# A recurrent attention followed by an MLP mixer: one more pair of weights formed in the second weave, and new orders for the first two

## The chip, the cores and the metric

The kernel runs on one core of a Trainium2 chip. A core has engines that run side by side, each with its own queue of instructions in order: TensorE (PE, matmuls; PEld is its loading of weights), VectorE (DVE), ScalarE (ACT), GpSimd (POOL) and SyncE (SP, which here issues nearly all DMA transfers). They wait for each other through semaphores only. The metric is the time of one execution on the device in microseconds (us), given as the median of several runs.

## The reference

For 4 batches of 768 tokens with 8 heads of 48 channels, a recurrence over time gives `y`; its heads side by side are `x` (768 x 384 per batch). Then an MLP mixer works along the tokens and along the channels:

```python
for t in range(S):
    cur = einsum(u * k_t, v_t);  y[t] = r_t @ (state + cur)
    state = w_t[:, None] * state + outer(k_t, v_t)
h  = relu(x.T @ w_tok1) @ w_tok2;   z = x + h.T       # 768 -> 256 -> 768 along the tokens
out = z + relu(z @ w_ch1) @ w_ch2                     # 384 -> 1536 -> 384 along the channels
```

The weights come as 64-bit floats and are turned into 32-bit ones on the chip.

## The kernel before

*Units and batches.* The attention of a batch is done in three units of 256 tokens (units 0 to 11 for four batches). A unit turns its decays into running products (`ends`, `begins`), scales keys and queries by them, forms grams of 64-token chunks on PE, carries the state from chunk to chunk, and copies its result into `x`. `own_u[a]` (L444, with `by_u` L327, the instruction of L329) multiplies the keys of one of four head pairs by `u` on ACT, for the diagonal of the gram.

*The mixing.* After the attention of a batch comes its mixing. For batch 0 (`mixing`, L880): `back` (L893; the matmuls of L896 and the residual add of L898 on DVE), `turn` (L903; three transposes on PE, L907, and a copy to `xT` by ACT, L909), `up` (L916; L931 and, for the last third of the tokens, L927, with a rectifying copy by ACT, L934 or L928) and `down` (L936; L942 and an add on DVE, L946). `up(s, jt)` works on the tokens of turns 2s and 2s+1. Batches 1 to 3 use `exact_mixing` (L635), whose matmuls take operands split in two shorter parts (L735, L737, L742 up; L753, L754, L755 down), with the first rectified part written by L717 on ACT.

*Conversion.* Each of the 64-bit channel weights comes as pairs of blocks; a pair is `load` (L257, SP), `signs` (L269, ACT), `exponent` (L260, DVE), `raise_two` (the power of two, L263, ACT), `mantissa` (L266), `add` (L272), and `put` (L275, L282), the last three on DVE.

*Forms.* The later mixings need each pair of channel weights in split forms. `splits(kind, n)` (L572) gives six pieces for pair `n` of the first (`kind` 0) or second (`kind` 1) weights: `up` (L575, ACT), `rest` (L579, DVE), `low` (L582, ACT), `store` (L588 or L590, a DMA on SP), `join` (L594, DVE), `joint` (L597, ACT). There are six pairs of each kind. The third form lies in DRAM and is loaded back into a ring of ten places (`load_third`, L615). The forms of the mixing's activations (`z_high`) lie in the room of the second channel weights, so L717 cannot write before the last `store` and `joint` of kind 1.

*The order.* Everything up to the first `back` is one list written out by hand (L1030). From there, four weaves follow, one per batch (L1135). A weave joins the mixing of a batch with the attention of the next and with what is left of the weights. Each of these is a list of pieces in a fixed order, a stream. A string of digits in `WEAVES` (L50) says from which stream the next piece is taken (`interleaved`, L1010), and `strict` (L103) makes every engine, SP among them, issue its instructions in that order. So a piece that waits for something holds up all that comes after it on its engine. In weave 0 the digits mean: 0 the mixing of batch 0, 1 to 3 the units 3, 4 and 5, 4 the rest of the conversion and the forms. In weave 1: 0 and 1 the mixing of batch 1 and the joins of its transposes, 2 to 4 the units 6 to 8, 5 the forms that are left. `weights_in_turn` (L1108) cuts the list of forms in two: the last 6 x `AFTER` pieces go into weave 1.

```python
    late = [e for n in range(HALF) for e in splits(1, n)]
    return first[:1] + each[1] + ... + formed + late[:1] + late[6:7] + late[1:6] + late[7:-6 * AFTER], late[-6 * AFTER:]
AFTER = 2
```

*Loads of keys.* `load_rk(i)` (L170) brings the keys and then the queries of a unit, each in two halves of 48 rows (the DMA of L168, on SP). The one for unit 3 stands near the end of the list by hand, behind two pairs of raw weights.

Of the kernel before, what the change touches and what calls it, by code (L numbers as in the profile page):

```python
# [47 lines left out]
LEAST, MOST = 2.0 ** -40, 2.0 ** 40  # L48
MID = 3 * G // 4 * SEG1
WEAVES = [  # L50
    "440140440440000440401041114001004140004404040411441110104414014401041041014144110144140104404110140444000414141004140414"
    "442044444104440214401040404000424420404012404240024022400042242242420242244422044040204442200422044422000202443003334030"
    "43040303443332342344343300343243434334034343243304404300344342403333",
    "050000022220000505250502225052502205522502012100010252000000220200002000200002200200020002000220300000300200330033003030"
    "033000000000030000023330330302000033303033003330000000101103000003300040020400000000204300000040044000444000404443304444"
    "4044040000000440404000400000044003040004040000300444000000000000",
    "204240000022033204220000433322344240400000044440010001100404440000000000044000004040040000400044004000400400404055550000"
    "050505000500000000055000450055450005055055540550500045005050500001101050505606000000000006000400000660606666065606060000"
    "066005066050606660000606000605600000606000600006060660006000000000000000",
# [6 lines left out]
def rwkv6_then_mixer(  # L66
# [1041 lines left out]
    def weights_in_turn():  # L1108
# [8 lines left out]
        late = [e for n in range(HALF) for e in splits(1, n)]  # L1117
        return first[:1] + each[1] + sum(each[2:], []) + stored + formed + late[:1] + late[6:7] + late[1:6] + late[7:-6 * AFTER], late[-6 * AFTER:]

    AFTER = 2  # L1120
    flagged = []

    def verdict():
# [153 lines left out]
```

## Time and profile before

| | |
|---|---|
| median of 3 runs | 483.54 us (482.88 to 484.61) |
| the profiled execution | 484.18 us, of which the span from first to last instruction is 482.4 us |
| mean clock granted to TensorE | 0.989 |
| DMA | 83.77 MB, 174 GB/s on average |

A profile shows for each engine the time that its instructions took (busy), and for idle time what released the engine. Rows of the form `start, duration, engine, line, operation, out<-in` stand for one instruction or for several alike (`xN`); a note in brackets gives the idle time ahead of it and what ended it. The rows by stage give, after the length of a stretch, the busy time of PE, PEld, DVE, ACT and POOL with the number of instructions, the clock granted to PE, and the share and rate of DMA. A 32-bit matmul leaves two records, one of shorter operands leaves one. Weave 0 runs from about 50 to 167 us, weave 1 to about 276 us.

### The profile page before, as it was taken

What the parts mean: (1) busy time and instruction counts of PE and PEld (TensorE: products, weight loads), DVE (VectorE), ACT (ScalarE), POOL (GpSimd) and SP (SyncE); (2) the same over time, 40 slices, a digit from 0 to 9 for tenths busy, and PEclk for the clock granted to TensorE, in tenths of its full rate; (3) what the DMA queues carried; (4) which work ended last, traced back from release to release, by engine and by line L of the source; (5) the groups of instructions that cost most, each with busy time, mean ns of one, the idle gap of its engine ahead of it and who ended that gap; (6) DMA issues with size and microseconds to landing.
All of it is one profiled execution on the core that took longest, in us unless ns stands there. A gap on an engine that the chain in (4) does not pass through costs nothing.

```text
span 482.4 us, 12668 instructions
## 1 busy us (share of the span) xinstructions
PE 464.6 (96%) x5298; PEld 407.8 (85%) x5298; DVE 336.4 (70%) x478; ACT 254.4 (53%) x587; POOL 59.3 (12%) x58
## 2 busy tenths in 40 slices
PE   3799999999999999999999999999999999999995
PEld 2686688866697668999999969999999979999994
DVE  7999899798788778757856398767856365235331
ACT  5789866753779666354546255365545244034040
POOL 1000000000000001230504002140413003032030
PEclk9889999999999999999999999999999999999998
DMA  8965927760674566774737644395605622436321
GB/s 300 336 200 205 271 96 244 254 209 33 190 239 136 187 176 209 211 225 150 228 129 242 224 146 127 116 262 182 194 23 177 219 77 83 123 91 206 90 81 56
DMA packets 49408, 83.77 MB, mean 174 GB/s; under 512 B 4864, under 2 KB 40576, under 8 KB 49344
## 3 DMA queue, kind: packets, MB, share of 16 engines
q1 hardware_dynamic: 49056, 82.80, 54.5%
q8 instruction: 43, 0.70, 0.6%
q14 instruction: 21, 0.17, 0.1%
q10 hardware_dynamic: 288, 0.10, 0.1%
HBM read 71.87 MB, written 11.01 MB: 172 GB/s over the span
## 4 chain that ended last, share of the span: by engine, by line
PE 95%; ACT 2%; DMA 1%; issue 0%; SPq 0%; DVE 0%; DVEq 0%; ACTq 0%
PE h_ps L942 10%; PE ends_ps L735 8%; PE ends_ps L742 8%; PE ends_ps L737 8%; PE o_ps L753 8%; PE o_ps L755 8%; PE o_ps L754 8%; PE z_ps L931 7%; PE h_ps L658 5%; PE gram L313 4%; PE z_ps L927 3%; PE h_ps L689 3%; PE kv_ps L361 3%; PE y_ps L397 3%; PE y_ps L376 2%; PE k_ps L343 2%
## 5 line engine op out<-in xcount | busy, mean ns | idle before, releaser
L728 POOL TENSOR_TENSOR z_high<-z_high 128x384 fp32r<-128x384 f32 x48 | 58.0, 1212 | 406.5 <-ACT z_high L717 188.9
L761 DVE SCALAR_TENSOR_TENSOR x<-o_ps,x 128x384 f32<-128x384 f32 x35 | 19.1, 555 | 55.5 <-PE o_ps L755 55.5
L717 ACT ACTIVATE z_high<-ends_ps 128x384 fp32r<-128x384 f32 x48 | 23.5, 489 | 58.1 <-PE ends_ps L742 58.1
L735 PE MATMUL ends_ps<-x_forms,forms 128*128 128x384 f32 x216 | 50.4, 341 | 0.0
L742 PE MATMUL ends_ps<-z_more,forms 128*128 128x384 f32 x216 | 50.2, 340 | 0.0
L737 PE MATMUL ends_ps<-x_forms,ring 128*128 128x384 f32 x216 | 49.3, 337 | 0.0
L942 PE MATMUL h_ps<-wch,z 128*128 128x384 f32 x144 | 48.6, 490 | 0.0
L724 DVE SCALAR_TENSOR_TENSOR z_high<-ends_ps,z_high 128x384 fp32r<-128x384 f32 x48 | 26.5, 553 | 31.0 <-ACT z_high L717 30.6
L753 PE MATMUL o_ps<-forms,z_high 128*128 128x384 f32 x140 | 47.9, 342 | 0.0
L755 PE MATMUL o_ps<-forms,z_high 128*128 128x384 f32 x140 | 47.2, 337 | 0.0
L754 PE MATMUL o_ps<-ring,z_high 128*128 128x384 f32 x140 | 47.1, 337 | 0.0
L497 ACT ACTIVATE before<-state,to_end 112x48 f32<-112x48 f32 x132 | 33.2, 323 | 18.2 <-DVE state L512 16.0
L942 PEld LDWEIGHTS h_ps<-wch,z 128*128 128x128 f32 x144 | 26.6, 190 | 16.8
L742 PEld LDWEIGHTS ends_ps<-z_more,forms 128*128 128x128 f32 x216 | 38.9, 188 | 0.3 <-DVE z_more L630 0.2
L735 PEld LDWEIGHTS ends_ps<-x_forms,forms 128*128 128x128 f32 x216 | 38.2, 188 | 0.7
L737 PEld LDWEIGHTS ends_ps<-x_forms,ring 128*128 128x128 f32 x216 | 38.6, 188 | 0.0
L931 PE MATMUL z_ps<-xT,wch 128*128 128x256 f32 x144 | 31.8, 380 | 0.0
L931 PEld LDWEIGHTS z_ps<-xT,wch 128*128 128x128 f32 x144 | 27.1, 190 | 3.8
L720 ACT ACTIVATE z_high<-z_high 128x384 fp32r<-128x384 f32 x48 | 25.2, 526 | 3.3
L753 PEld LDWEIGHTS o_ps<-forms,z_high 128*128 128x128 f32 x140 | 26.3, 188 | 0.2
L754 PEld LDWEIGHTS o_ps<-ring,z_high 128*128 128x128 f32 x140 | 26.3, 188 | 0.0
L755 PEld LDWEIGHTS o_ps<-forms,z_high 128*128 128x128 f32 x140 | 26.3, 188 | 0.0
(194 smaller groups left out, 929.4 us busy)
## 6 DMA issues: line engine op xcount, KB each, us to landing
ring<-third SPq DMA_DIRECT2D x144, 192.0 KB, 3.2
raw<-in_w_ch_dram SPq DMA_DIRECT2D x16, 512.0 KB, 5.0
rk<-in_rk_dram SPq DMA_DIRECT2D x36, 192.0 KB, 5.2
near<-in_near_dram SPq DMA_DIRECT2D x8, 768.0 KB, 4.9
w<-in_w_dram SPq DMA_DIRECT2D x10, 520.5 KB, 4.0
vt<-in_v_dram SPq DMA_DIRECT2D x12, 384.0 KB, 4.4
out_dram<-x SPq DMA_DIRECT2D x17, 192.0 KB, 2.3
third<-forms SPq DMA_DIRECT2D x12, 192.0 KB, 3.3
```

The lines of the kernel that those rows point to most:

```text
L497: act.mul(t[:ROWS, a], state[bt, g][:ROWS, a], by_last(c, j)[:, a:a + 1])
L720: act.mul(z_form(jt, 2), z_form(jt, 0).bitcast(f32), 1.0 / BASE)
L724: dve.scalar_tensor_tensor(z_form(jt, 1), a, 0.0, z_form(jt, 0).bitcast(f32), op0=ALU.max, op1=ALU.subtract)
L728: pool.tensor_add(z_form(jt, 2), z_form(jt, 2).bitcast(f32), z_form(jt, 1).bitcast(f32))
L735: pe.matmul(a, up[m], xf[0][:, m], start=m == 0, stop=False)
L737: pe.matmul(a, low[:, m], xf[1][:, m], start=False, stop=False)
L742: pe.matmul(banks["a", jt], joint, xf[2][:, m], start=False, stop=m == 2)
L753: pe.matmul(a, z[0], up, start=first, stop=False, skip_group_check=True)
L754: pe.matmul(a, z[1], held[bt, s, half, 1, jt], start=False, stop=False, skip_group_check=True)
L755: pe.matmul(a, z[2], joint, start=False, stop=last, skip_group_check=True)
L931: pe.matmul(ps, now["wch1"][:, m, ts(jt, 128)], xT[:, m, ts(s, SEG)], start=(m == 0), stop=(m == DM // 128 - 1))
L942: pe.matmul(ps, zs[s][:, jt, ts(n, 128)], now["wch2"][:, jt, :], start=(jt == 0), stop=(jt == NJ - 1))
```

## The change

`AFTER` goes from 2 to 3: pair 3 of the second channel weights, the third from the end, has its six pieces in weave 1 instead of weave 0. The strings of weaves 0 and 1 are replaced as a whole (that of weave 0 has 302 digits instead of 308, that of weave 1 310 instead of 304; weaves 2 and 3 are untouched). No piece is added or removed.

```diff
 WEAVES = [
-    "440140440440000440401041114001004140004404040411441110104414014401041041014144110144140104404110140444000414141004140414"
...
+    "114444104104040410004140000400004414400001444004414111110414014404040014140414110441144010144440101014440011441040411001041"
...
-    "050000022220000505250502225052502205522502012100010252000000220200002000200002200200020002000220300000300200330033003030"
...
+    "000255552050020225500050020220552050550125022520510252125002000000200000020020000002020000000202200200022020000330300000"
...
-    AFTER = 2
+    AFTER = 3
```

At the start of weave 0 this changes the order on two engines. On PE it stays `back` 0 to 2, `turn` 0, `back` 3, `turn` 1, `back` 4, `turn` 2, `back` 5, `turn` 3, `up`. On the others:

| engine | before | after |
|---|---|---|
| ACT | signs 1, power 1, copy of turn 0, turn 1, signs 2, copy of turn 2, own_u[0] of unit 3, copy of turn 3, power 2, own_u[1], [2], [3], first rectified copies | own_u[0] of unit 3, signs 1, power 1, own_u[1], [2], copy of turn 0, turn 1, own_u[3], signs 2, copy of turn 2, turn 3, first rectified copies, power 2 |
| DVE | put 0, add of back 0, exponent 1, back 1, mantissa 1, back 2, add 1, back 3, back 4, put 1, exponent 2, back 5 | put 0, exponent 1, back 0, mantissa 1, back 1, add 1, back 2, back 3, put 1, back 4, back 5, exponent 2 |

Later in weave 0, units 4 and 5 run somewhat earlier beside the matmuls of `down` and `up` (their `tokens`, `carry` and grams move by a few matmuls of L942 and L927), and unit 5 is finished before the last two pieces of `down`. In weave 1 the six pieces of pair 3 stand near the start, behind the loads of unit 6 and among the first matmuls of L658; pairs 4 and 5 follow. On SP the store of pair 3 then comes ahead of the first four loads of the ring.

More of the change, by code (lines that the diff above doesn't have):

```diff
@@ L50 @@
 WEAVES = [
-    "440140440440000440401041114001004140004404040411441110104414014401041041014144110144140104404110140444000414141004140414"
-    "442044444104440214401040404000424420404012404240024022400042242242420242244422044040204442200422044422000202443003334030"
-    "43040303443332342344343300343243434334034343243304404300344342403333",
-    "050000022220000505250502225052502205522502012100010252000000220200002000200002200200020002000220300000300200330033003030"
-    "033000000000030000023330330302000033303033003330000000101103000003300040020400000000204300000040044000444000404443304444"
-    "4044040000000440404000400000044003040004040000300444000000000000",
+    "114444104040410004140000400004414400001444004414111110414014404040014140414110441144010144440101014440011441040411001041"
+    "444040420414440424100242440201244222024404444040420022244220442402424204042204420242442000400402224434034004404042300034"
+    "03304334033434343423333333332033400344300343304243344424300033",
+    "000255552050020225500050020220552050550125022520510252125002000000200000020020000002020000000202200200022020000330300000"
+    "023033300000003303000030003233030300330330233003303230003000002300110034100400000004000000400444034004004040000434340004"
+    "0344044440040040400004004000004044300040000400004000440000000000000000",
     "204240000022033204220000433322344240400000044440010001100404440000000000044000004040040000400044004000400400404055550000"
```

## The prediction

> **What bounds the kernel now.** I read the page first, then who waited for whom on PE, then the busy time by stage.
>
> ```profile
> span 482.4 us, 12668 instructions
> ...
> PE 464.6 (96%) x5298; PEld 407.8 (85%) x5298; DVE 336.4 (70%) x478; ACT 254.4 (53%) x587; POOL 59.3 (12%) x58
> ...
> PE 95%; ACT 2%; DMA 1%; issue 0%; SPq 0%; DVE 0%; DVEq 0%; ACTq 0%
> ...
> PE gram L313 <- DMA rk<-in_rk_dram: 8.4, 1, 8.4
> PE kv_ps L504 <- ACT before L497: 1.2, 2, 1.0
> PE k_ps L343 <- PE kv_ps L504: 0.8, 1, 0.8
> PE h_ps L896 <- ACT h L891: 0.6, 1, 0.6
> PE y_ps L397 <- ACT seen L385: 0.5, 1, 0.5
> PE h_ps L689 <- ACT z_high L682: 0.2, 1, 0.2
> ...
> 60.00:70.00 10.00, 10.00 (x52) 8.75 (x50) 9.90 (x13) 7.08 (x15) 0.00 (x0) 1.00 0.38 126
> ...
> 165.00:187.00 22.00, 22.00 (x262) 14.35 (x262) 16.91 (x23) 13.06 (x24) 0.00 (x0) 1.00 0.64 187
> ```
>
> PE is the chain (95% of it). All its waits together are 11.7 us, and all but the last belong to the first 50 us, which the change leaves alone: on every engine the first moved instruction stands behind them. In the two woven stages (about 50 to 167 and 167 to 276 us) the rows by stage show PE busy for 10.00 of 10.00 and 22.00 of 22.00 us. Busy can hide gaps between pipelined matmuls, so I looked at their spacing:
>
> ```profile
> 58.99 10.36 PE z_ps L931 x48
> ...
> 101.85 10.52 PE h_ps L942 x32
> ```
>
> 0.216 us each for 128x256 and 0.329 for 128x384, the same wherever they stand. So there is hardly a wait to take away: what the new order can win on PE is about the 0.2 us of L689. What it can lose is open: a wait that PE is now given is lost to the end, because nothing behind it has slack on PE.
>
> The Trainium skill, "Perfetto Trace Analysis", Identifying the Most-Contended Engine, says that matmul busy time tells little of headroom and that the share of weight loading should be read instead. By that rule the stage of 165 to 187 us (weight loading 14.35 of 22) would have up to 7.65 us to win; the even spacing above speaks against it, and it enters only as a rival below.
>
> **The change, part by part.** *The moved pair.* AFTER = 3 takes the six pieces of pair 3 of the second channel weights (up L575, rest L579, low L582, store L590, join L594, joint L597) out of the first weave and puts them into the second.
>
> ```profile
> L575 ACT ACTIVATE forms<-wch 128x768 fp32r<-128x768 f32 x12 | 10.0, 839 | 2.7 <-DVE starts L427 2.6
> L579 DVE TENSOR_TENSOR forms<-wch,forms 128x768 fp32r<-128x768 f32 x12 | 11.2, 944 | 0.6 <-ACT forms L575 0.6
> L582 ACT ACTIVATE wch<-forms 128x768 f32<-128x768 f32 x6 | 5.0, 841 | 2.6 <-DVE forms L579 2.2 <-PE h_ps L942 0.3
> L594 DVE TENSOR_TENSOR forms<-forms,wch 128x768 fp32r<-128x768 f32 x6 | 5.7, 954 | 1.0 <-ACT wch L582 0.9
> ...
> 180.90 0.37 SPq L590 DMA_DIRECT2D third<-wch  x1
> ...
> DMA to landing us min/median/max: 2.4/3.6/5.5
> ...
> 188.88 0.47 ACT L717 ACTIVATE z_high<-ends_ps 128x384 fp32r<-128x384 f32 x1
> ```
>
> That is 3 x 0.84 = 2.5 us of ACT, 0.94 + 0.95 = 1.9 us of DVE and one store of 384 KB. In the first weave they lay beside PE, so taking them out wins nothing. In the second, between 165 and 187 us, ACT goes from 13.06 to 15.6 and DVE from 16.91 to 18.8 of 22 us: they fit. What would be late if they did not is the first L717: its tile lies in the room of the second channel weights, so it waits for the last store, issued at 180.90; with the 3.6 us that the six stores of L590 took in the median it landed at 184.5, 4.4 us before 188.88. An extra pair put wholly ahead of that store costs 0.84 + 0.94 + 0.84 = 2.6 us, and with join and joint 4.4: even so L717 is not late, and I take 0. (If that cover were gone, the same 4.4 us would be the price.) On SP the store goes ahead of the first loads of the ring (L621) and delays their issue by its own 0.37 us.
>
> *The order of PE, DVE and SP elsewhere.* Both programs have the same matmuls, and 36 places in each where a run of 64-row matmuls gives way to full ones; the new order on PE costs 0. On DVE the exponent of conversion 1 (L260) now precedes the first residual add (L898).
>
> ```profile
> 51.40 1.22 DVE L282 SCALAR_TENSOR_TENSOR wch<-z 128x1024 f32<-128x1024 f32 x1
> 52.55 0.54 DVE L898 TENSOR_TENSOR x<-x,h_ps 128x384 f32<-128x384 f32 x1
> 53.01 0.69 DVE L260 TENSOR_SCALAR raw<-raw 128x1024 uint16<-128x1024 uint16 x1
> ```
>
> L260 costs 0.6 us (53.01 to the next start), so the first add starts at 53.15 instead of 52.55 and the first transpose on PE, which followed 53.54 when PE was free, starts 0.1 to 0.2 us late. That is swallowed by the next wait.
>
> *The start of the first weave on ACT.* This is the term that counts. In the order of before, ACT does: signs of conversion 1 (L269), its power of two (L263), the copies of turns 0 and 1 (L909), signs of conversion 2, the copy of turn 2, own_u[0] of unit 3 (L329), the copy of turn 3. In the new order own_u[0] stands first of all, and own_u[1], [2] and [3] also come ahead of the copies of turns 0, 2 and 3. own_u reads the keys of unit 3, which the SP queue loads late:
>
> ```profile
> L168 SPq DMA_DIRECT2D rk<-in_rk_dram x2: 438/444/450, 45.1 to 45.6; - x2
> ...
> DMA to landing us min/median/max: 8.4/8.6/8.8
> ...
> L168 SPq DMA_DIRECT2D rk<-in_rk_dram x8: 310/366/450, 45.1 to 53.1; - x8
> ...
> DMA to landing us min/median/max: 5.3/8.8/9.4
> ...
> 51.82 1.17 ACT L423 ACTIVATE junk<-to_end,most 112x1041 uint8<-112x1041 f32 x1
> 52.89 0.19 ACT L423 ACTIVATION_READ_ACCUMULATOR junk<-to_end,most 112x1 f32 x1
> 52.98 1.15 ACT L269 ACTIVATE first<-raw 128x1024 bf16<-128x1024 int32 x1
> 54.04 1.13 ACT L263 ACTIVATE raw<-raw,rebias 128x1024 uint16<-128x1024 uint16 x1
> 55.08 0.46 ACT L909 COPY xT<-xT_ps 128x384 f32<-128x384 f32 x1
> ...
> 59.02 0.48 ACT L909 COPY xT<-xT_ps 128x384 f32<-128x384 f32 x1 [0.73 <-PE xT_ps L907]
> ...
> 61.19 1.29 ACT L329 ACTIVATE near<-rk,u_col 112x256 f32<-112x256 f32 x3
> ...
> 58.82 4.48 PE L931 MATMUL z_ps<-xT,wch 128*128 128x256 f32 x20
> ...
> 8.30 0.14 issue
> ```
>
> The two halves of the keys were issued at 45.1 and 45.6 us and landed 8.4 and 8.8 us later: the second at 54.4. Nothing ahead of these loads changes on SP, so I keep that time. A waiting engine starts up to 0.14 us after a landing (8.30 to 8.44). ACT, free at 52.98, then stands still until 54.56: 1.6 us, with its whole queue behind it. From there by start-to-start times: own_u[0] 0.42 (54.98), signs 1.06 (56.04), power 1.04 (57.08), own_u[1] and [2] 0.4 each (57.88), copies of turns 0 and 1 0.4 each (58.68), own_u[3] 0.4 (59.08), signs 1.06 (60.14), copy of turn 2 0.4 (60.54), copy of turn 3 0.48: done at about 61.0.
>
> PE needs that last copy for up(1, 0), the third and fourth matmul of L931 (each is two records): before, it began at 58.82 + 4 x 0.216 = 59.68, with the copy done at 59.50, so PE had under 0.2 us to spare. Now it begins at 61.0 plus the 0.18 us of a weight load that no longer hides (8.75 us for 50 in the row of 60 to 70): 61.2. PE loses 1.5 us. Were the keys there at 52.98, the same queue would end at 59.4, no later than before: a loss of 0, which holds if the load takes the shortest 5.3 us of the eight; with their longest, 9.4, the wait grows by 0.6 and the loss to 2.1. I take 1.5, nearest to the rows of the two loads themselves. The others behind this queue lose nothing: the signs of conversion 1 are ready at 56.1 and its power at 57.2, and DVE and SP, busy with what stands ahead, ask for them only after that.
>
> **The sum.** 482.4 of span + 1.5 + 0 + 0 = 483.9, with the 1.8 us around the span (484.18 in all) 485.7 for a profiled execution. That one lay 0.64 us above the median 483.54, so the forecast for the median is 485.0 us, that is 0.3% over before. About 0.3%, 1.45 us, is also what a measurement of this kernel can tell from no change: its runs reach from 482.88 to 484.61.
>
> **The rivals.** *The keys are there in time (not slower).* The loads wait behind four raw loads of 512 KB in a busy queue; unprofiled, or with a slightly different start, they may land earlier. Every microsecond earlier than 54.4 takes one off the loss; from about 52.9 on it is 0, and the time stays 483.5; a time up to 484.0 I count here. Against it: the SP order up to there is unchanged, and the loads took 8.4 and 8.8 us.
>
> *The clock falls.* The wait would leave PE busy for 1.9 us of the 3.4 from 58.75 on.
>
> ```profile
> 14.38:17.79 3.41, 2.40 (x117) 1.97 (x109) 3.41 (x3) 2.00 (x10) 0.00 (x0) 1.00 1.06 367
> 17.79:21.20 3.41, 2.46 (x46) 1.85 (x46) 3.41 (x5) 1.43 (x6) 0.00 (x0) 1.00 0.97 359
> 21.20:24.62 3.42, 2.89 (x71) 2.26 (x70) 3.33 (x4) 3.42 (x12) 0.00 (x0) 0.50 0.67 241
> 48.51:51.93 3.42, 2.84 (x9) 1.44 (x8) 1.74 (x3) 3.23 (x6) 0.00 (x0) 1.00 1.05 311
> ```
>
> After two stretches at 2.40 and 2.46 the clock was halved; one at 2.84 left it whole. One stretch at 1.9 between full ones lies beyond what the rows decide. If it fell for two stretches (6.8 us) PE would lose half of them: 485.0 + 3.4 = 488.4. The Trainium skill, "TensorE: Matmul & The Clock Gate", Part 1, says that the clock is throttled after a window of about 3.4 us that is idle; by that rule a wait of 1.5 us leaves it whole and the time stays 485.0. The trace agrees only in part, since no stretch of 3.4 us before 21.2 was idle.
>
> *The second weave does not hold the extra pair.* Stores of L590 took 2.4 to 5.5 us; one of 5.5 instead of 3.6, with everything in series, makes L717 1.9 us late, and PE with it once its PSUM banks are used up: 485.0 + 1.9 = 486.9. Against it: DVE has 3.2 us left over there.
>
> *Faster.* If matmuls had the headroom that weight loading suggests, a better mix could show it; half of the 7.65 us that the rule gives would be 485.0 - 3.8 = 481.2. The spacing rows leave 0.2 us.
>
> **Chances.** Forecast (485.0, own range 484.3 to 485.9) 0.62; keys in time 0.17; clock 0.08; second weave 0.08; faster 0.05. Of the forecast's share I put 0.36 above the bound of 484.99 and 0.26 below. So slower 0.36 + 0.16 = 0.52, within 0.26 + 0.17 = 0.43, faster 0.05. The range reaches down to 483.1 (keys in time, and as much below as its runs scatter) and up to 487.4 (second weave); the clock and the gain stay out.
>
> **What would show it.** In the changed profile: ACT idle for about 1.6 us up to a first L329 at about 54.6, released by the load of rk; the copy of turn 3 done at about 61; a new PE wait of z_ps L931 for ACT L909 of 1.2 to 1.6 us; PEclk 1.00 from 60 to 70; no new PE wait between 165 and 200 us. It is wrong if L329 starts before 53.5, or if PE waits elsewhere by more than 0.5 us.

## The result, and the profile after

| | before | after | ratio, 95% interval |
|---|---|---|---|
| median of 5 runs each, those of before with the three shown above among them | 484.34 us (482.88 to 484.73) | 486.69 us (486.36 to 486.75) | 1.0043 [1.0024, 1.0063] |
| the profiled execution: span | 482.4 us | 484.9 us | |
| clock granted to TensorE | 0.989 | 0.991 | |

The changed kernel is slower by 0.43%, 2.1 us by that ratio; forecast were 485.0 us and a loss of 1.5 us, in a range of 483.1 to 487.4. The 486.69 us lie above the forecast's own range of 484.3 to 485.9, inside the wider one. The ratio is worked out from all the runs, here and below, and is not the quotient of the two medians. The page of the changed kernel, with its chain:

```profile
PE 89%; DMA 6%; ACT 3%; DVE 1%; SPq 1%; issue 0%; DVEq 0%; ACTq 0%
```

DMA has gone from 1% to 6% and PE from 95% to 89%, so the chain now leaves PE somewhere and follows a transfer. Where, the waits of PE from 50 us on tell (waiting instruction, what it waited for, us in total, times, longest):

```profile
PE z_ps L931 <- ACT xT L909: 0.8, 1, 0.8
PE h_ps L896 <- ACT h L891: 0.6, 1, 0.6
PE h_ps L689 <- ACT z_high L682: 0.2, 1, 0.2
```

The second and third were there before; the first is new, and it is the only new one behind 50 us. Here is ACT's timeline around it in the changed kernel (start, duration, engine, line, operation, out<-in; in brackets the idle time ahead and its releaser):

```profile
54.29 0.19 ACT L423 ACTIVATION_READ_ACCUMULATOR junk<-to_end,most 112x1 f32 x1
55.84 0.51 ACT L329 ACTIVATE near<-rk,u_col 112x256 f32<-112x256 f32 x1 [1.36 <-DMA rk<-in_rk_dram]
56.25 1.15 ACT L269 ACTIVATE first<-raw 128x1024 bf16<-128x1024 int32 x1
...
58.35 0.89 ACT L329 ACTIVATE near<-rk,u_col 112x256 f32<-112x256 f32 x2
59.15 0.83 ACT L909 COPY xT<-xT_ps 128x384 f32<-128x384 f32 x2
59.88 0.51 ACT L329 ACTIVATE near<-rk,u_col 112x256 f32<-112x256 f32 x1
60.29 1.14 ACT L269 ACTIVATE first<-raw 128x1024 bf16<-128x1024 int32 x1
61.32 0.85 ACT L909 COPY xT<-xT_ps 128x384 f32<-128x384 f32 x2
```

ACT stands still for 1.36 us until the keys have landed, then runs without a pause, and the copy of turn 3 ends at 61.32 + 0.85 = 62.17. PE, first as it was before (its first `back`), then after:

```profile
49.66 4.14 PE L896 MATMUL h_ps<-h,wtok 128*128 128x384 f32 x12 [0.58 <-ACT h L891]
```

```profile
51.06 4.14 PE L896 MATMUL h_ps<-h,wtok 128*128 128x384 f32 x12 [0.58 <-ACT h L891]
...
60.39 1.03 PE L931 MATMUL z_ps<-xT,wch 128*128 128x256 f32 x4
62.22 4.15 PE L931 MATMUL z_ps<-xT,wch 128*128 128x256 f32 x18 [0.80 <-ACT xT L909]
```

The four records of up(0, 0) are issued; up(1, 0) would follow after 4 x 0.216 us, at 61.25, and comes at 62.22. That is 0.97 us, of which the view of waits shows 0.80, since it counts from the modelled end of the fourth record (60.39 + 1.03).

The 2.5 us by which the spans differ can be split in two. PE begins the first `back` 1.40 us later (51.06 to 49.66), in a part where both programs are the same; and from there to the start of up(1, 0) it needs 62.22 - 51.06 = 11.16 instead of 59.69 - 49.66 = 10.03 us, 1.13 more. Behind that point nothing is lost: 484.9 - 62.22 = 422.7 us, and before 482.4 - 59.69 = 422.7. So the pair in the second weave and all later reordering weigh nothing in this execution; what had to be shown is whether the 1.13 us is the wait for the keys, and whose the 1.40 is.

### The profile page after: what moved, and what is told of

It is laid out like the page before. It is cut to its first block, busy times and chain, and to the rows that moved or that the text cites. A ratio compares the mean times of both kernels' runs of the same rounds, so it can differ in the third digit from the quotient of the medians.

```text
span 484.9 us, 12662 instructions
## 1 busy us (share of the span) xinstructions
PE 465.9 (96%) x5298; PEld 408.2 (84%) x5298; DVE 337.3 (70%) x478; ACT 254.5 (52%) x587; POOL 61.3 (13%) x58
## 3 DMA queue, kind: packets, MB, share of 16 engines
q1 hardware_dynamic: 49056, 82.80, 54.4%
## 4 chain that ended last, share of the span: by engine, by line
PE 89%; DMA 6%; ACT 3%; DVE 1%; SPq 1%; issue 0%; DVEq 0%; ACTq 0%
PE h_ps L942 10%; PE ends_ps L735 8%; PE ends_ps L742 8%; PE ends_ps L737 8%; PE o_ps L753 8%; PE o_ps L755 8%; PE o_ps L754 8%; PE z_ps L931 6%; PE h_ps L658 5%; PE gram L313 3%; PE z_ps L927 3%; PE h_ps L689 3%; PE kv_ps L361 2%; PE y_ps L397 2%; PE y_ps L376 2%; PE h_ps L698 2%
## 5 line engine op out<-in xcount | busy, mean ns | idle before, releaser
L728 POOL TENSOR_TENSOR z_high<-z_high 128x384 fp32r<-128x384 f32 x48 | 60.0, 1256 | 407.1 <-DVE z_high L724 354.9
L717 ACT ACTIVATE z_high<-ends_ps 128x384 fp32r<-128x384 f32 x48 | 23.5, 490 | 68.5 <-PE ends_ps L742 67.8
L942 PE MATMUL h_ps<-wch,z 128*128 128x384 f32 x144 | 48.7, 490 | 0.0
L942 PEld LDWEIGHTS h_ps<-wch,z 128*128 128x128 f32 x144 | 26.6, 190 | 16.8
L931 PE MATMUL z_ps<-xT,wch 128*128 128x256 f32 x144 | 32.0, 381 | 0.8 <-ACT xT L909 0.8
L931 PEld LDWEIGHTS z_ps<-xT,wch 128*128 128x128 f32 x144 | 27.0, 190 | 4.8 <-ACT xT L909 1.2
```

What stands on the lines that cost most here:

```text
L728: pool.tensor_add(z_form(jt, 2), z_form(jt, 2).bitcast(f32), z_form(jt, 1).bitcast(f32))
L931: pe.matmul(ps, now["wch1"][:, m, ts(jt, 128)], xT[:, m, ts(s, SEG)], start=(m == 0), stop=(m == DM // 128 - 1))
L942: pe.matmul(ps, zs[s][:, jt, ts(n, 128)], now["wch2"][:, jt, :], start=(jt == 0), stop=(jt == NJ - 1))
```

## The experiments

All were timed beside the kernel before, in two groups, each on one chip: the undo, the cause alone, the keys earlier and the wait alone (median of before 484.51 us, 30 runs), and the other four (484.63 us, 23 runs).

### The undo: `own_u` put back

In the changed kernel, own_u[0] of unit 3 goes back ahead of turn 3 and own_u[1] to [3] behind it. AFTER = 3 and everything else stay.

```diff
-    "114444104040410004140000400004414400001444004414111110414014404040014140414110441144010144440101014440011441040411001041"
+    "144440404040004400010111400004414400001444004414111110414014404040014140414110441144010144440101014440011441040411001041"
```

> The changed kernel with own_u[0] to [3] of unit 3 put back on ACT behind the copy of turn 2 (own_u[0]) and of turn 3 (the others); the rest of both new weaves stays. Theory A (ACT is held by the load of the keys with the four own_u ahead of the copies, and PE waits for the copy of turn 3): the loss goes, 484.3 us, ratio to before 0.999 to 1.001, no PE wait of L931 for L909. Rival B (of the 2.5 us between the two profiles 1.4 lie in the first 50 us, which are the same program; the loss is half there): 485.4 to 485.7. Rival C (the loss comes from the rest of the two weaves, the moved pair among it): 486.5.

Measured: 484.18 us, ratio 1.0005 [0.9987, 1.0024]. In its timelines of ACT and PE the copy of turn 3 again waits for PE, and the row of L931 (35 records) has no pause:

```profile
58.82 0.48 ACT L909 COPY xT<-xT_ps 128x384 f32<-128x384 f32 x1 [0.73 <-PE xT_ps L907]
```

```profile
49.29 4.14 PE L896 MATMUL h_ps<-h,wtok 128*128 128x384 f32 x12 [0.58 <-ACT h L891]
...
58.62 7.72 PE L931 MATMUL z_ps<-xT,wch 128*128 128x256 f32 x35
```

The loss is gone with the four pieces alone. What remains, the moved pair and all other reordering, costs 0.17 us ahead of up(1, 0) (10.20 against 10.03 us from PE's first `back`) and nothing behind it (table below); the timed interval reaches up to 1.0024, so the time alone could not say that much.

### The cause alone: `own_u` moved in the kernel before

The kernel before, AFTER = 2, with own_u[0] to [3] moved forward as the change does it; nothing else.

```diff
-    "440140440440000440401041114001004140004404040411441110104414014401041041014144110144140104404110140444000414141004140414"
+    "114404041404410000414040044001004140004404040411441110104414014401041041014144110144140104404110140444000414141004140414"
```

> The kernel before, AFTER = 2 and weave 1 untouched, with only own_u[0] to [3] of unit 3 moved as far forward on ACT as in the change. Theory A: the whole loss appears, 486.4 to 486.8, with the PE wait of L931 for L909. Rival B: about 485.5. Rival C: 484.3, since none of the rest of the weaves is there.

Measured: 487.85 us, ratio 1.0076 [1.0049, 1.0104].

```profile
57.04 0.51 ACT L329 ACTIVATE near<-rk,u_col 112x256 f32<-112x256 f32 x1 [2.65 <-DMA rk<-in_rk_dram]
...
62.49 0.85 ACT L909 COPY xT<-xT_ps 128x384 f32<-128x384 f32 x2
```

```profile
50.98 4.14 PE L896 MATMUL h_ps<-h,wtok 128*128 128x384 f32 x12 [0.58 <-ACT h L891]
...
60.84 0.55 PE L907 MATMUL xT_ps<-ident,x 128*128 128x128 f32 x3 [0.86 <-ACT xT L909]
61.23 1.12 PE L931 MATMUL z_ps<-xT,wch 128*128 128x256 f32 x4
63.40 2.86 PE L931 MATMUL z_ps<-xT,wch 128*128 128x256 f32 x12 [1.05 <-ACT xT L909]
```

The four pieces by themselves make the whole loss. It is larger here than the 486.4 to 486.8 us expected, because the keys landed later against PE: 57.04 - 50.98 = 6.06 us after the first `back`, where the changed kernel had 4.78. The later ACT runs, the more waits appear on PE: the transposes of turn 3 already wait for the copy of an earlier turn (0.86), before up(1, 0) waits for that of turn 3 (1.05).

### The keys earlier

The changed kernel, with the load of unit 3's keys one place ahead in the list by hand, in front of a pair of raw weights.

```diff
-  h[9], add3, behind(e1["tokens"], to_ch[2][0]), ... product2, lambda: load_rk(3), put2)
+  h[9], add3, lambda: load_rk(3), behind(e1["tokens"], to_ch[2][0]), ... product2, put2)
```

> The changed kernel with the load of unit 3's keys and queries issued ahead of the second pair of raw channel weights, two transfers of 512 KB earlier on SP; the order of the pieces in the weaves stays. Theory A: the keys are there before ACT asks, ACT does not stand still, 484.2 to 484.6. Rival B: 485.4 to 485.7. Rival C: 486.5. If the reordered own_u alone (without the wait) cost PE, 485.0 to 485.5 with ACT busy through from 53 to 61 us.

Measured: 485.11 us, ratio 1.0026 [1.0003, 1.0049].

```profile
53.56 0.49 ACT L329 ACTIVATE near<-rk,u_col 112x256 f32<-112x256 f32 x1
...
58.71 1.16 ACT L269 ACTIVATE first<-raw 128x1024 bf16<-128x1024 int32 x1 [0.62 <-DMA raw<-in_w_ch_dram]
59.77 0.84 ACT L909 COPY xT<-xT_ps 128x384 f32<-128x384 f32 x2
```

```profile
50.23 4.14 PE L896 MATMUL h_ps<-h,wtok 128*128 128x384 f32 x12 [0.58 <-ACT h L891]
...
60.67 0.48 PE L931 MATMUL z_ps<-xT,wch 128*128 128x256 f32 x1
```

With the keys there, the same order of ACT has no wait for them, and the view of PE's waits shows none for the copies. Not all of the time came back, for the raw weights are now the late ones (signs of conversion 2 wait 0.62 us, the copies end at 60.61, and up(1, 0) starts at 60.67, 0.2 us late against 59.57 + 0.87, where 59.57 is the start of L931). The time is above the 484.2 to 484.6 us of the theory and inside the 485.0 to 485.5 that were set down for pieces that cost by themselves. That reading asked for an ACT busy from 53 to 61 us, which it is not, and the three pieces alone, below, speak against it. The interval neither holds 1 nor leaves out the changed kernel's own ratio, so the time by itself decides little; the profile does.

### The wait alone

The kernel before, with only the loads and own_u[0] moved to the head of the weave; own_u[1] to [3] stay behind turn 3.

```diff
-    "440140440440000440401041114001004140004404040411441110104414014401041041014144110144140104404110140444000414141004140414"
+    "114404044044000044040041114001004140004404040411441110104414014401041041014144110144140104404110140444000414141004140414"
```

> The kernel before with own_u[0] alone moved to the head of the weave on ACT; own_u[1] to [3] stay behind the copy of turn 3. It has the wait for the keys but three instructions (1.2 us) less ahead of the copies. Theory A by its sum: the copy of turn 3 ends 1.2 us earlier than with all four, the loss over before is 0.3 to 1.0 us, 484.6 to 485.3. If the wait for the load counts whole whatever follows: 486.0 or more. If only the number of instructions ahead of the copies counts: 484.3.

Measured: 484.80 us, ratio 1.0007 [0.9989, 1.0025].

```profile
53.95 0.51 ACT L329 ACTIVATE near<-rk,u_col 112x256 f32<-112x256 f32 x1 [1.39 <-DMA rk<-in_rk_dram]
...
58.23 0.86 ACT L909 COPY xT<-xT_ps 128x384 f32<-128x384 f32 x2
```

```profile
49.14 4.14 PE L896 MATMUL h_ps<-h,wtok 128*128 128x384 f32 x12 [0.58 <-ACT h L891]
...
58.30 8.02 PE L931 MATMUL z_ps<-xT,wch 128*128 128x256 f32 x36
```

ACT waits 1.39 us, as in the changed kernel (1.36), with the first `own_u` the same 4.8 us behind PE's first `back`, and PE loses nothing: the copy of turn 3 ends at 59.09, up(1, 0) starts at 58.30 + 0.87 = 59.17. The wait by itself fits into the slack that ACT's queue had, if only just (59.09 against 59.17). The loss of 0.3 to 1.0 us that was expected here is not in the profile; the timed interval would allow either.

### The three pieces alone

The mirror of that: in the changed kernel no `own_u` stands ahead of the signs any more; the first now follows the power of conversion 1. Three of them still come ahead of the copies of turns 0 and 2, the fourth between those of turns 2 and 3, so ahead of the copy of turn 3 there are three more than in the kernel before.

```diff
-    "114444104040410004140000400004414400001444004414111110414014404040014140414110441144010144440101014440011441040411001041"
+    "144441040404100041400010400004414400001444004414111110414014404040014140414110441144010144440101014440011441040411001041"
```

> The changed kernel with one edit: no own_u stands ahead of signs 1 on ACT; the first now comes behind the power of conversion 1 (three own_u still come ahead of the copies of turns 0 and 2, and the fourth between the copies of turns 2 and 3). Theory (it takes both, the wait for the keys at the head of the queue and the pieces put ahead of the copies; the wait alone cost nothing in the run with only the first own_u moved): by start-to-start times signs 52.98, power 54.04, own_u 55.08 and 55.48, copies 55.9 and 56.3, own_u 56.7, signs 57.1, copy 58.2, own_u 58.6, copy of turn 3 done at 59.5, as before the change: 484.2 to 484.8 us; if the keys land as late as in the profile of the changed kernel (55.74) up to 0.7 us of the loss stays (485.3). Rival (the three pieces ahead of the copies cost by themselves, 3 x 0.4 us, whenever the keys land): 485.6. Rival (the loss is elsewhere): 486.7.

Measured: 484.81 us, ratio 1.0001 [0.9984, 1.0019].

```profile
55.52 0.89 ACT L329 ACTIVATE near<-rk,u_col 112x256 f32<-112x256 f32 x2
...
59.65 0.48 ACT L909 COPY xT<-xT_ps 128x384 f32<-128x384 f32 x1 [0.28 <-PE xT_ps L907]
```

```profile
50.11 4.14 PE L896 MATMUL h_ps<-h,wtok 128*128 128x384 f32 x12 [0.58 <-ACT h L891]
...
59.45 6.86 PE L931 MATMUL z_ps<-xT,wch 128*128 128x256 f32 x31
```

No wait for the keys, none on PE; ACT even waits for PE again (0.28). The rival that the three pieces cost 1.2 us wherever the keys are asked for 1.0025 and is outside the interval. So neither part costs by itself; it takes both.

### The keys later

The changed kernel, with the queries of unit 3 loaded ahead of its keys.

```diff
-            for n in (1, 0):
+            for n in (0, 1) if i == UB else (1, 0):
```

> The changed kernel with one edit: for unit 3 the queries are loaded ahead of the keys, so that the two halves of the keys are issued two DMA issues (about 0.9 us) later and land behind the queries; everything else as in the changed kernel. Theory (ACT stands still for the keys at the first L329, and its queue holds the copy of turn 3 that PE needs): ACT waits about 1 to 1.5 us longer, the copies of turns 2 and 3 come that much later, PE's wait for ACT L909 grows from 0.8 to 1.8 to 2.3 us (part of it may show at L907), and the time goes from 486.7 to 487.7 to 488.2 us. Rival 1 (the loss sits in the new order of the weaves later on, or in the pair moved to the second weave): 486.7, unchanged. Rival 2 (the loss sits in the first 50 us): 486.7 give or take 0.5, with no larger wait for L909.

Measured: 487.63 us, ratio 1.0067 [1.0039, 1.0094].

```profile
56.02 0.51 ACT L329 ACTIVATE near<-rk,u_col 112x256 f32<-112x256 f32 x1 [2.59 <-DMA rk<-in_rk_dram]
```

```profile
50.01 4.14 PE L896 MATMUL h_ps<-h,wtok 128*128 128x384 f32 x12 [0.58 <-ACT h L891]
...
60.18 1.13 PE L931 MATMUL z_ps<-xT,wch 128*128 128x256 f32 x4 [0.68 <-ACT xT L909]
62.37 3.94 PE L931 MATMUL z_ps<-xT,wch 128*128 128x256 f32 x17 [1.05 <-ACT xT L909]
```

ACT's wait is 1.2 us longer than in the first profile of the changed kernel and 0.6 longer than in its second, and PE now waits for the copies twice, 0.68 + 1.05 = 1.73, a little less than the 1.8 forecast. The median is about where the theory put it, but its interval overlaps that of the changed kernel, so it is the timeline that speaks here.

### Both kernels once more

> The changed kernel once more, for a second profile of the same program: theory: ACT waits at the first L329 again, PE waits for ACT L909 again (0.5 to 2 us, by when the keys land), and the time is 486.4 to 487.0 us. If the difference of 1.4 us that the two profiles show in the first 50 us, where both programs are the same, belongs to one execution, it is another here; if it belongs to the changed kernel, it is there again: PE reaches the first L896 at 51.0 rather than 49.7.

> The kernel before once more, for a second profile of the same program: the keys land between 53 and 56 us, PE has no wait for ACT L909, and PE reaches the first L896 anywhere from 49.6 to 51.0 if the first 50 us differ from one execution to the next, at 49.7 if they do not.

Measured: the changed kernel 486.23 us, ratio 1.0037 [1.0016, 1.0057]; the kernel before 484.08 us in its one run. The changed kernel's second profile:

```profile
55.50 0.51 ACT L329 ACTIVATE near<-rk,u_col 112x256 f32<-112x256 f32 x1 [2.00 <-DMA rk<-in_rk_dram]
```

```profile
50.08 4.14 PE L896 MATMUL h_ps<-h,wtok 128*128 128x384 f32 x12 [0.58 <-ACT h L891]
...
61.86 4.37 PE L931 MATMUL z_ps<-xT,wch 128*128 128x256 f32 x19 [1.05 <-ACT xT L909]
```

and the second of the kernel before:

```profile
49.71 4.14 PE L896 MATMUL h_ps<-h,wtok 128*128 128x384 f32 x12 [0.58 <-ACT h L891]
...
58.87 7.50 PE L931 MATMUL z_ps<-xT,wch 128*128 128x256 f32 x34
```

PE reached its first `back` at 50.08, 1.0 us earlier than in the first profile of the same program. So most of the 1.40 us does not belong to the program, while the wait for the keys came back, and larger.

### All ten executions in one table

The columns: PE's first L896; the first `own_u` on ACT, from there, where it is one of the first things in the queue; the time from the first L896 to up(1, 0); and what is left from there to the end of the span (all us). up(1, 0) is the fifth record of L931, the row that follows a wait where there is one; without a wait it comes 0.87 us behind the start of L931 (by the single records, good to 0.01), and for the keys earlier it is 60.67.

| execution | first L896 | first `own_u` | L896 to up(1, 0) | up(1, 0) to end |
|---|---|---|---|---|
| before | 49.66 | | 10.03 | 422.7 |
| before, again | 49.71 | | 10.03 | 422.6 |
| the wait alone | 49.14 | +4.81 | 10.03 | 422.6 |
| the undo | 49.29 | | 10.20 | 422.6 |
| the three pieces alone | 50.11 | | 10.20 | 422.6 |
| the keys earlier | 50.23 | +3.33 | 10.44 | 422.5 |
| after | 51.06 | +4.78 | 11.16 | 422.7 |
| after, again | 50.08 | +5.42 | 11.78 | 422.6 |
| the keys later | 50.01 | +6.01 | 12.36 | 422.6 |
| the cause alone | 50.98 | +6.06 | 12.42 | 422.7 |

Two columns settle the case. The last: behind up(1, 0) all ten executions take 422.5 to 422.7 us, whether pair 3 lies in the first weave or in the second and whichever strings order the weaves. The others: with all four pieces ahead and the keys late, the third column follows the second one for one (from +4.78 to +6.06 is 1.28 us, from 11.16 to 12.42 is 1.26); with one part missing it stays at 10.0 to 10.2, or 10.4 in the keys earlier, where the raw weights made a wait of their own.

In these four executions up(1, 0) comes 6.35 to 6.38 us after ACT's first `own_u`, whenever PE began its first `back`. So as long as PE waits, the keys set, by way of ACT's queue, when it goes on, and a PE that is behind only waits less: given the keys of the first profile, the 1.40 us did not lengthen its span. In absolute time the changed kernel reached up(1, 0) at 62.22 and 61.86 us, the kernel before at 59.69 and 59.74, which is 2.1 to 2.5 us.

## Why the prediction was right, point by point

*The chain.* That PE was the chain with nothing to win held: from 49 us on PE's waits in the kernel before were those of L896 and L689, and no variant won any of it.

*The moved pair, taken at 0.* It costs 0: the undo keeps it at a ratio of 1.0005, and the last column of the table has no place for it. In the stretch that answers to 165 to 187 us (moved by the 2.5 us that PE is behind), DVE had 18.19 us, where 18.8 had been forecast, and ACT 12.51 instead of 15.6. All of pair 3's pieces lie in it (on ACT from L575 at 167.80 to L597 at 175.61), but the `joint` of pair 3 lay in the old stage too (165.63), so only two pieces of 0.84 us came in, and of the copies of the attention's result into `x` (L403) one is left in it where there were four (0.5 instead of 1.9 us). The stage in the changed kernel, then the last store on SP with its time to landing, then the first L717 on ACT:

```profile
167.50:189.50 22.00, 22.00 (x203) 14.15 (x202) 18.19 (x24) 12.51 (x21) 0.00 (x0) 1.00 0.59 178
```

```profile
L590 SPq DMA_DIRECT2D third<-wch x1: 370/370/370, 186.6 to 186.6; - x1
...
DMA to landing us min/median/max: 2.7/2.7/2.7
```

```profile
191.32 0.49 ACT L717 ACTIVATE z_high<-ends_ps 128x384 fp32r<-128x384 f32 x1 [0.41 <-ACT before L497]
```

The last store landed 2.7 us after its issue, at 189.3, so 2.0 of the 4.4 us of cover are left. L717 follows 2.44 us behind its time before, no more than PE itself.

*The order of DVE, taken at 0.1 to 0.2 us and swallowed by the wait.* The variants with the change's order of DVE and no wait show it by itself: 10.20 against 10.03 us, 0.17. (In the working the first transpose of before is put at 53.54; the trace has it at 53.64.) In the changed kernel it lies ahead of the wait and is swallowed, as forecast.

*The start of the first weave, taken at 1.5 us.* The mechanism was right, each step of it: ACT idle at a first L329 released by the keys, copies behind it, a new wait of L931 for L909. That the pieces cost nothing without the wait was in the working too, since its sum with the keys at 52.98 was a loss of 0; that the wait would cost nothing without the pieces was not, and the run with the wait alone still expected a loss. The size in the profiles, against PE's own start, was 1.13 and 1.75 us, on either side of the 1.5 forecast. The steps behind it were less exact than that: the keys were taken to land at 54.4 on the ground that nothing ahead of them changes on SP, and ACT began at 55.84 and 55.50; PE was behind as well, by 1.40 and 0.42 us, so that most of this cancelled. That is luck: what sets this loss is the landing against PE's own position, and the working had derived neither shift. The chain from the first L329 to the end of the copy was taken as 6.4 us (54.56 to 61.0) and was 6.33, and the weight load that no longer hides took 0.05 instead of 0.18 us. The others behind this queue were taken to lose nothing; in the changed kernel DVE did wait 0.25 us for the power of conversion 1 (L275 at 58.47), and PE lost nothing by it.

*The sum, 485.0 us.* Measured were 486.69 and 486.23. For a profiled execution the working gave a span of 483.9 us, with up(1, 0) at 61.2; the spans were 484.9 and 484.5, with up(1, 0) at 62.22 and 61.86, so it is the late keys that are missing there. The absolute median is off for two reasons. The base: the median of before was 483.54 in the runs that were shown, and 484.34, 484.51 and 484.63 in the comparisons, 0.8 to 1.1 us more. And the ratios 1.0043 and 1.0037 make 2.1 and 1.8 us, where the profiles make 1.13 and 1.75 against PE's own start and 2.5 and 2.1 in absolute time. Both intervals hold the 1.5 us forecast (1.0031). How much of the timed loss goes with the start of PE stays open, since one run of each set was profiled. That the median fell inside the outer range was helped by its upper end, 487.4, which was put there for a rival, the second weave, that did not come about.

*The rivals.* Keys in time: not so; they came 1.36 and 2.00 us after ACT was free. The clock: it stayed whole. Stages across the wait, in the second profile of the changed kernel and then, with the longest wait of all, in the cause alone:

```profile
58.75:62.17 3.42, 2.31 (x10) 1.28 (x9) 3.39 (x6) 3.06 (x7) 0.00 (x0) 1.00 0.70 279
```

```profile
58.75:62.17 3.42, 2.56 (x11) 1.37 (x9) 2.67 (x5) 3.42 (x7) 0.00 (x0) 1.00 0.75 258
62.17:65.59 3.42, 2.37 (x11) 1.96 (x11) 3.39 (x5) 2.77 (x6) 0.00 (x0) 1.00 0.15 62
65.59:69.00 3.41, 3.41 (x18) 3.00 (x17) 3.34 (x6) 0.99 (x3) 0.00 (x0) 1.00 0.28 35
```

PE was busy for 2.31 of 3.42 us, or for 2.56 and 2.37 in two stretches on end, and the granted clock is 1.00 there and behind. The Trainium skill, "TensorE: Matmul & The Clock Gate", Part 1, has the clock fall after a window in which PE is idle; these rows agree with it, while the fall at 21.20 in the kernel before, after stretches at 2.40 and 2.46, still does not. The working's remark that no stretch of 3.4 us before 21.2 was idle is wrong: PE was busy for 0.00 of the first 7.55 us there, and the granted clock shows as 1.00 from the start up to 21.20. The second weave and the gain: no trace of either.

## What to carry to other kernels

Where every engine issues in a fixed order, ask of each piece that moves forward what it waits for, and add that wait to the work that it pushes ahead of others: here a wait of 1.4 us cost nothing, three short pieces cost nothing, and both together cost 1.1 us and more, because only then was the slack of ACT's queue used up. To see what a reordering costs, cut the span at the first point behind it and compare the two parts: if the rest is equal to 0.2 us, as here in ten executions, everything later is cleared at one stroke. A time of landing taken from one execution is good to a microsecond or two. Compare it with the position of the engine that will be kept waiting, which moves as well.

## What was not expected of the hardware

The same stretch of program came out differently from one execution to the next. PE's first `back` began between 49.14 and 51.06 us in the ten profiles, which have the same matmuls up to there. The granted clock does not tell it: its mean was 0.999 in the undo and 0.991 in the wait alone, where PE was earliest, at 49.29 and 49.14. In the first profile of the changed kernel part of it is a pause inside the last fourteen records of L888 that no semaphore explains; it is put down to issue:

```profile
44.86 1.56 PE L888 MATMUL h_ps<-x,wtok 128*128 128x384 f32 x4
46.99 3.49 PE L888 MATMUL h_ps<-x,wtok 128*128 128x384 f32 x10 [0.57 <-issue]
```

In its second profile the same fourteen ran on without a pause:

```profile
44.72 4.78 PE L888 MATMUL h_ps<-x,wtok 128*128 128x384 f32 x14
```

By the spacing of 0.329 us the pause is 0.8 us (44.86 + 4 x 0.329 = 46.18). The same pause, as long and at the same place, stands in the profile of the three pieces alone, where the first four records begin at 43.89:

```profile
46.04 3.49 PE L888 MATMUL h_ps<-x,wtok 128*128 128x384 f32 x10 [0.59 <-issue]
```

What made it was not tried. The loads of the keys varied as well: the two halves were issued at 44.2 and 44.8 us and landed after 10.7 and 10.9 us in the first profile of the changed kernel, and at 45.3 and 45.8 and after 9.3 and 9.6 us in its second (those of before: 8.4 and 8.8). Why is left open.
